# A second set of decoding buffers and eight more weight tiles for the first block of a fused attention, convolution and MLP kernel

## The chip, the cores and the metric

The kernel runs on one core of a Trainium2 chip. The metric is the device time of one execution in microseconds; the time before is the median of three runs, 1207.55 us (1206.89 to 1210.84). The engines are TensorE (PE, matmuls and transposes), VectorE (DVE), ScalarE (ACT), GpSimd (POOL) and SyncE (SP), which issues most of the DMAs here.

## What is computed

Three stages one after the other over 8 x 576 = 4608 tokens of width 512: attention within chunks of 64 tokens, a gated causal convolution, and a normalised two-layer network with a residual. Inputs q, k, v and g_ln are float32. All the weights are float64, because they are multiplied by a numpy scalar. In short form:

```
scores = scale * np.matmul(q_c, k_c.transpose(0, 1, 2, 4, 3))      # chunks of 64
attn = np.exp(scores - np.max(scores, axis=-1, keepdims=True))
attn = attn / (np.sum(attn, axis=-1, keepdims=True) + 1e-09)
x = heads_to_columns(np.matmul(attn, v_c))                        # 8 x 576 x 512
gate_pre += conv_w[k][None, None, :] * xp[:, k:k + S, :]          # k = 0..4
gate = 1.0 / (1.0 + np.exp(-gate_pre))
y = (gate * (x @ w_val)) @ w_out
xn = (y - mu) / np.sqrt(var + 1e-06) * g_ln
out = y + np.maximum(xn @ w_ch1, 0.0) @ w_ch2                     # hidden width 2048
```

## The kernel before

**Weights.** A float64 weight arrives as pairs of 32-bit words. decode (line 103) makes a float32 of each: one ACT operation on the high word (L106) and three integer operations on DVE (L107, L108, L109). split (line 111) then makes the two parts that PE multiplies, in fp32r: a rounded copy on ACT (L114) and the remainder by a subtraction on POOL (L115). Each product of two matrices is three matmuls, high by high, high by low and low by high. The raw words lie in the pool stg under the tag "raw" (two buffers), the decoded tile under the tag "da" (three buffers). The rows that the normalisation reads (load_rows, line 335) use the tag "da" too.

**Stages.** The tokens are cut into 36 units of 128 and nine blocks of 512. slot(u) (line 585) issues the loads of q, k and v of unit u+2, transposes q and k of unit u, and finishes unit u-2. The convolution, the value product and the output product of a block (tile names cg, psv, pso) are handed out over the slots that follow it, by the table dense. The order of PE in the first seven slots is that of the code (manual schedule); later a planner places the instructions. Behind slot(2), cwr takes the decoded convolution weights (20 rows) and g_ln (4 rows), and one transpose turns them into cw, which the convolution reads (L613 to L617).

After the last unit, prep(t) for t=0 to 3 normalises the rows of block 0 in pairs (ln_pair, line 341) into xn0, loads yt0 (the same rows, for the residual), and loads and splits the weight pairs f=0 to 3 of the network (load_ff, split_ff). A pair f is 128 of the 2048 hidden columns: w1 of it (512 x 128) and w2 of it (128 x 512).

**First block.** The loop at L673 runs over the 16 hidden tiles: ff1(0, f) is 12 matmuls psh<-xn,w, then hh on ACT and hl on DVE; ff2(0, f-1) is 12 matmuls into four accumulators acc. Behind them stands load_ff/split_ff of f+4. The w1 tiles turn over in four places of wA, so w1 of f+4 takes the place of w1 of f. Each decoded w1 tile is also stored to a scratch tensor (ad, L154). At f=4, 6, 8 and 10 ln_pair normalises two of the eight tiles of rows of the next two blocks into xt.

**Pairs.** The other eight blocks go two at a time (s=0 to 3) through eight pairs of hidden tiles; each pair is seven products of half matrices (zy, x) in place of eight, from seven sums of the weights (wc, built by make_pair from the scratch tensor) and seven right-hand operands (b21, b11, b22, t1 to t4, built in place on xt by right_operands, pool xb). Here the order of PE is that of the code again.

SP issues in its own order, one instruction after the other, and an instruction that waits for a buffer holds what is behind it.

## Time and profile before

| | us |
|---|---|
| median of three runs | 1207.55 |
| lowest, highest | 1206.89, 1210.84 |
| the profiled execution | 1211.44 |
| its span (first to last instruction) | 1209.7 |
| PE busy | 1124.9 (93%) |
| DVE busy | 739.4 (61%) |
| ACT busy | 529.6 (44%) |
| POOL busy | 159.8 (13%) |

The profile's times are from the start of the span. In a row of a timeline the first number is the start, the second the time that the row's instructions took, xN how many there are, and the brackets name how long the engine stood idle ahead of it and what ended that. "out<-in" are tile names. PEclk is the granted clock of TensorE as a share of its full 2.4 GHz.

### The profile page before, as it was taken

Reading aid. Unit: us, or ns where it says so; the run is one execution under the profiler, and the core shown is the slowest. Engines: PE = TensorE matmul, PEld = TensorE weight load, DVE = VectorE, ACT = ScalarE, POOL = GpSimd, SP = SyncE. Lnnn points to the kernel's source line nnn. Section 1 sums busy time; section 2 is a strip of 40 time slices with the busy share of each in tenths; the row PEclk is TensorE's granted clock in tenths of the full one; section 3 lists DMA queues with packets and bytes.
Section 4 is the critical chain, followed back from the end, with each engine's and each line's share of the span. In section 5 each row is a group of like instructions: output and inputs, shape, how many; then the busy total and the mean of one; then the engine's idle time right before and its main releaser. Section 6 shows DMA issues by size and latency. Waiting matters only on the chain.

```text
span 1209.7 us, 18324 instructions
## 1 busy us (share of the span) xinstructions
PE 1124.9 (93%) x7127; PEld 903.8 (75%) x7127; DVE 739.4 (61%) x1244; ACT 529.6 (44%) x973; POOL 159.8 (13%) x160
## 2 busy tenths in 40 slices
PE   6689999999999977769999999999999999999998
PEld 5567777777777754547888778888888887887876
DVE  6688898888885776575554654343844436543333
ACT  4467677677666445443443422332323423222221
POOL 2131131111112322333231000000000000000000
PEclk8789999999999988789999999999999999999999
DMA  7745664444024553454343263323443332622212
GB/s 181 177 98 146 187 181 119 114 121 123 36 70 141 181 168 112 158 198 174 122 140 122 87 227 105 105 97 107 156 162 105 120 106 79 234 88 87 88 36 78
DMA packets 168908, 155.37 MB, mean 128 GB/s; under 512 B 120670, under 2 KB 128886, under 8 KB 168822
## 3 DMA queue, kind: packets, MB, share of 16 engines
q1 hardware_dynamic: 163638, 144.76, 39.5%
q10 hardware_dynamic: 5184, 9.44, 2.1%
q8 instruction: 56, 0.92, 0.3%
q14 instruction: 30, 0.25, 0.1%
HBM read 116.41 MB, written 37.75 MB: 127 GB/s over the span
## 4 chain that ended last, share of the span: by engine, by line
PE 49%; DVE 5%; DMA 2%; POOL 1%; issue 1%; ACT 1%; SPq 0%; POOLq 0%; DVEq 0%; ACTq 0%
PE acc L497 13%; PE x L522 13%; PE psf L497 13%; PE zy L522 8%; DVE h L532 1%; POOL wc L407 1%; DVE xt L459 1%; PE pst L365 1%; DMA raws<-ad 1%; DVE yt L502 1%; DMA yr<-yd 1%; DVE t L407 1%; DMA out<-yr 0%; ACT h L531 0%; PE acc L399 0%
## 5 line engine op out<-in xcount | busy, mean ns | idle before, releaser
L540 DVE TENSOR_TENSOR c<-x,c 128x512 f32<-128x512 f32 x96 | 66.2, 689 | 234.4 <-ACT c L536 179.9
L497 PE MATMUL acc<-w,h 128*128 128x512 f32 x768 | 186.1, 391 | 0.0
L497 PE MATMUL psf<-w,h 128*128 128x512 f32 x768 | 186.0, 391 | 0.0
L497 PEld LDWEIGHTS acc<-w,h 128*128 128x128 f32 x768 | 144.2, 188 | 31.4
L497 PEld LDWEIGHTS psf<-w,h 128*128 128x128 f32 x768 | 144.2, 188 | 31.3
L522 PE MATMUL x<-t,wc 128*128 128x512 f32 x576 | 148.3, 393 | 3.3 <-DVE c L540 3.3
L536 ACT ACTIVATE c<-zy 128x512 f32<-128x512 f32 x96 | 57.9, 604 | 193.2 <-PE zy L522 193.1
L522 PEld LDWEIGHTS x<-t,wc 128*128 128x128 f32 x576 | 108.8, 189 | 27.9 <-DVE c L540 4.6
L531 ACT ACTIVATE h<-c 128x512 fp32r<-128x512 f32 x96 | 60.5, 631 | 133.5 <-DVE c L540 133.1
L276 DVE SCALAR_TENSOR_TENSOR cg<-xf,cw,cg 128x516 f32<-128x516 f32 (+1 forms) x176 | 117.7, 716 | 0.3
L522 PE MATMUL zy<-b,wc 128*128 128x512 f32 x384 | 100.5, 397 | 2.1 <-ACT wc L406 1.9
L502 DVE TENSOR_TENSOR yt<-psf,yt 128x512 f32<-128x512 f32 x128 | 88.0, 690 | 23.0 <-PE psf L497 19.1
L522 PEld LDWEIGHTS zy<-b,wc 128*128 128x128 f32 x384 | 71.7, 190 | 18.0 <-ACT wc L406 2.4
L532 DVE SCALAR_TENSOR_TENSOR h<-c,h 128x512 fp32r<-128x512 f32 x96 | 68.4, 713 | 12.4 <-ACT h L531 12.1
L264 POOL TENSOR_TENSOR xl<-xf,xh 128x512 fp32r<-128x512 f32 (+1 forms) x40 | 51.3, 1287 | 164.1 <-ACT xh L263 164.1
L290 PE MATMUL pso<-oh,gh 128*128 128x512 f32 x144 | 60.0, 416 | 8.2 <-ACT gh L307 5.8
L290 PE MATMUL psv<-xh,vh 128*128 128x512 f32 x144 | 59.9, 417 | 5.3 <-DVE gv L304 4.0
L115 POOL TENSOR_TENSOR w<-da,w 128x512 fp32r<-128x512 f32 x32 | 46.0, 1440 | 123.2 <-ACT w L114 93.4
L407 POOL TENSOR_TENSOR wc<-raws,wc 128x256 fp32r<-128x256 f32 x56 | 47.5, 871 | 103.6 <-ACT wc L406 103.4
L290 PE MATMUL psv<-xl,vh 128*128 128x512 f32 x144 | 58.2, 404 | 0.8 <-POOL xl L264 0.8
L290 PE MATMUL psv<-xh,vl 128*128 128x512 f32 x144 | 58.1, 403 | 0.0
L522 PE MATMUL zy<-t,wc 128*128 128x512 f32 x192 | 50.9, 400 | 6.9 <-ACT wc L406 6.5
(108 smaller groups left out, 1799.7 us busy)
## 6 DMA issues: line engine op xcount, KB each, us to landing
wc<-wc SPq DMA_DIRECT2D x112, 512.0 KB, 3.2
raw<-in_moe_w_ch SPq DMA_DIRECT2D x32, 512.0 KB, 3.9
yr<-yd SPq DMA_DIRECT2D x52, 256.0 KB, 3.3
vr<-in_v SPq DMA_DIRECT2D x144, 64.0 KB, 2.5
yd<-y ACTq DMA_DIRECT2D x36, 256.0 KB, 2.8
kr<-in_k SPq DMA_DIRECT2D x64, 128.0 KB, 2.9
qr<-in_q SPq DMA_DIRECT2D x64, 128.0 KB, 2.9
out<-yt SPq DMA_DIRECT2D x20, 256.0 KB, 3.1
```

The lines of the kernel that those rows point to most:

```text
L115: (eng or nc.gpsimd).tensor_tensor(out=lo, in0=a, in1=hi, op=ALU.subtract)
L264: nc.gpsimd.tensor_tensor(out=xl[j][:, :, lo:hi], in0=src, in1=xh[j][:, :, lo:hi], op=ALU.subtract)
L276: nc.vector.scalar_tensor_tensor(out=o, in0=x[:, f, i + lo:i + hi], scalar=cw[:, i * CT + f:i * CT + f + 1], in1=o, op0=ALU.mult, op1=ALU.add,
L290: nc.tensor.matmul(out=ps, lhsT=lt, rhs=rh, start=(i == 0), stop=(i == n - 1))
L407: eng.tensor_tensor(out=lo, in0=a, in1=hi, op=ALU.subtract)
L497: nc.tensor.matmul(out=ps, lhsT=lt, rhs=rh, start=(g == 0 and k == 0 and (first or half)), stop=(g == 1 and k == 2 and (last or half)),)
L502: nc.vector.tensor_tensor(out=yt[i], in0=ps, in1=yt[i], op=ALU.add)
L522: nc.tensor.matmul(out=ps, lhsT=lt, rhs=rh, start=(start and c == 0 and i == 0), stop=(c == 1 and i == 2), skip_group_check=True)
L531: nc.scalar.activation(out=t[:, 0, :], in_=src, func=ACTF.Relu)
L532: nc.vector.scalar_tensor_tensor(out=t[:, 1, :], in0=src, scalar=0.0, in1=t[:, 0, :], op0=ALU.max, op1=ALU.subtract)
L536: nc.scalar.activation(out=t, in_=zy, func=ACTF.Copy)
L540: nc.vector.tensor_tensor(out=t, in0=x, in1=t, op=ALU.add)
```

## The change

- g_ln gets a tile of its own, gr, in the pool of constants. It is loaded right behind the convolution weights, ahead of the loads of unit 2, and transposed by a second small transpose. cwr then holds the 20 rows of the convolution alone.
- A second pool of staging buffers, stg2, with raw and da tiles of its own (two each), takes the odd f from f=5 on. The even f stay in stg.
- w1 of f=4 to 7 go to a new pool w1p and those of f=12 to 15 to a new pool w3p; f=0 to 3 and 8 to 11 share the four places of wA. These pools and stg2 hold memory that the right-hand operands (xb) use later; they are closed behind ff2 of f=15, and xb opens then. It used to open ahead of the loop.
- The loop runs two more pairs ahead: next_ff(4) and next_ff(5) stand before it, and next_ff(f+6) in it.
- ln_pair becomes ln_rows, which takes its rows. Block 0 is normalised in one call of four tiles, from yt0 itself; yt0 is overwritten by that and loaded a second time. For xt, each pair of tiles has a tile "y" of its own in stg2, at f=3, 5, 7 and 9.
- make_pair(0) stands ahead of right_operands(), and both outside the manual order.
- split loses the choice of engine for the subtraction, which was always POOL.

The core of the diff:

```diff
+    gr = const.tile([CT, P], F32, name="gr")
...
-    def split(hi, lo, raw, eng=None):
-        a = stg.tile([P, DM], F32, tag="da", name="da", bufs=3)
+    def split(hi, lo, raw, pool=None):
+        a = (pool or stg).tile([P, DM], F32, tag="da", name="da", bufs=3)
...
-    def load_ff(f):
-        r1 = stg.tile([P, DM, 2], U32, tag="raw", name="raw1")
+    def load_ff(f, pool):
+        r1 = pool.tile([P, DM, 2], U32, tag="raw", name="raw1", bufs=2)
...
-    def split_ff(f):
+    def split_ff(f, pool):
         r1, r2 = wraw.pop(f)
-        t = wA.tile([P, 2, DM], F32R, tag=f"s{NFA + f % NFA}", name=f"w0_{f}")
-        a = split(t[:, 0, :], t[:, 1, :], r1)
+        g, m = divmod(f, NFA)
+        if g % 2 == 0:
+            t = wA.tile([P, 2, DM], F32R, tag=f"s{NFA + m}", name="w0")
+        else:
+            t = p2[f"w{g}"].tile([P, 2, DM], F32R, tag=f"w{m}", name="w0")
+        a = split(t[:, 0, :], t[:, 1, :], r1, pool)
...
-    def ln_pair(s, i):
-
-        ys = [load_rows(s, i + t) for t in range(2)]
+    def ln_rows(ys, i):
...
+    nc.sync.dma_start(out=gr, in_=g_ln.rearrange("(c p) -> c p", p=P))
...
-    cwr = stg.tile([(KC + 1) * CT, P], F32, tag="da", bufs=3, name="cwr")
-    nc.sync.dma_start(out=cwr[KC * CT:(KC + 1) * CT, :], in_=g_ln.rearrange("(c p) -> c p", p=P))
-    decode(cwu, cwr[0:KC * CT, :])
+    cwr = stg.tile([KC * CT, P], F32, tag="da", bufs=3, name="cwr")
+    decode(cwu, cwr)
     ps = ps_t.tile([P, NP * P], F32, tag="t", name="pst")
-    nc.tensor.transpose(out=ps[:, 0:(KC + 1) * CT], in_=cwr, identity=ident[0:(KC + 1) * CT, 0:(KC + 1) * CT])
+    nc.tensor.transpose(out=ps[:, 0:KC * CT], in_=cwr, identity=ident[0:KC * CT, 0:KC * CT])
+    nc.tensor.transpose(out=ps[:, KC * CT:(KC + 1) * CT], in_=gr, identity=ident[0:CT, 0:CT])
...
-            nc.sync.dma_start(out=yt0, in_=y_dram[0].rearrange("(t p) d -> p t d", p=P))
-        if t % 2 == 0:
-            ln_pair(-1, t)
-            src = p2["xt"][:, :, t * P:(t + 2) * P]
-            hi, lo = (x[:, :, t * P:(t + 2) * P] for x in xn0)
-            nc.scalar.activation(out=hi, in_=src, func=ACTF.Copy)
-            nc.vector.tensor_tensor(out=lo, in0=src, in1=hi, op=ALU.subtract)
-        load_ff(t)
-        split_ff(t)
+            y0 = y_dram[0].rearrange("(t p) d -> p t d", p=P)
+            nc.sync.dma_start(out=yt0, in_=y0)
+            ln_rows([yt0[:, i, :] for i in range(HB)], 0)
+            nc.sync.dma_start(out=yt0, in_=y0)
+            for i in range(0, HB, 2):
+                ts = slice(i * P, (i + 2) * P)
+                high_low(xn0[0][:, :, ts], xn0[1][:, :, ts], p2["xt"][:, :, ts], nc.vector)
+        load_ff(t, stg)
+        split_ff(t, stg)
...
-    p2["xb"] = ctx.enter_context(tc.tile_pool(name="xb", bufs=1, reuse_waits="tile"))
+    s_1 = ExitStack()
+    p2["w1"] = s_1.enter_context(tc.tile_pool(name="w1p", bufs=1, reuse_waits="tile"))
+    stg2 = s_1.enter_context(tc.tile_pool(name="stg2", bufs=2, reuse_waits="tile"))
+    p2["w3"] = s_1.enter_context(tc.tile_pool(name="w3p", bufs=1, reuse_waits="tile"))
+
+    def next_ff(f):
+        if NFA <= f < NF:
+            pool = stg2 if f % 2 else stg
+            load_ff(f, pool)
+            split_ff(f, pool)
+
+    def rows_of(s, i, t):
+        for k in range(2):
+            nc.sync.dma_start(out=t[:, k, :], in_=rows(s, i + k)[0])
+        return [t[:, k, :] for k in range(2)]
+
+    next_ff(NFA)
+    next_ff(NFA + 1)
     for f in range(NF):
         ff1(0, f)
         if f > 0:
             ff2(0, f - 1)
-        if f + NFA < NF:
-            load_ff(f + NFA)
-            split_ff(f + NFA)
-        if f in (4, 6, 8, 10):
-            ln_pair(0, f - 4)
+        next_ff(f + NFA + 2)
+        if f in (3, 5, 7, 9):
+            ln_rows(rows_of(0, f - 3, stg2.tile([P, 2, DM], F32, tag="y", name="yr")), f - 3)
     ff2(0, NF - 1)
-    right_operands()
+    s_1.close()
+    p2["xb"] = ctx.enter_context(tc.tile_pool(name="xb", bufs=1, reuse_waits="tile"))
     s_0.close()
     p2["hr"] = ctx.enter_context(tc.tile_pool(name="p2r", bufs=5, side="right", reuse_waits="tile"))
     p2["wx"] = ctx.enter_context(tc.tile_pool(name="p2w", bufs=1, side="right", reuse_waits="tile"))
     p2["c"] = ctx.enter_context(tc.tile_pool(name="pc", bufs=2, reuse_waits="tile"))
     p2["yt"] = ctx.enter_context(tc.tile_pool(name="pyt", bufs=2, reuse_waits="tile"))
+    make_pair(0)
+    right_operands()
     order = ExitStack()
     order.enter_context(tc.manual_schedule(engines={mybir.EngineType.PE}))
-    make_pair(0)
```

SP at the head, from the load of the convolution weights (cwu) on: the loads of units 2, 3 and 4, and g_ln. Before:

```order
L575 DMA cwu<-in_moe_conv_w 20x256
L88 DMA kr<-in_k 128x4x64 x2
L88 DMA qr<-in_q 128x4x64 x2
L97 DMA vr<-in_v 64x4x64 x4
L88 DMA kr<-in_k 128x4x64 x2
L88 DMA qr<-in_q 128x4x64 x2
L97 DMA vr<-in_v 64x4x64 x4
L88 DMA kr<-in_k 64x4x64 x4
L88 DMA qr<-in_q 64x4x64 x4
L97 DMA vr<-in_v 64x4x64 x4
L613 DMA cwr<-in_moe_g_ln 4x128
```

After:

```order
L579 DMA cwu<-in_moe_conv_w 20x256
L580 DMA gr<-in_moe_g_ln 4x128
L89 DMA kr<-in_k 128x4x64 x2
L89 DMA qr<-in_q 128x4x64 x2
L98 DMA vr<-in_v 64x4x64 x4
L89 DMA kr<-in_k 128x4x64 x2
L89 DMA qr<-in_q 128x4x64 x2
L98 DMA vr<-in_v 64x4x64 x4
L89 DMA kr<-in_k 64x4x64 x4
L89 DMA qr<-in_q 64x4x64 x4
L98 DMA vr<-in_v 64x4x64 x4
```

The load of g_ln moved from behind the loads of three units (32 instructions) to a place ahead of them.

DVE in the first block, between the hl of f=1 and that of f=2. Before, raw1_4936 and raw2_4938 are the weights of f=4:

```order
L384 SCALAR_TENSOR_TENSOR hl_4971<-psh_4957,hh_4970 128x512
L109 SCALAR_TENSOR_TENSOR da_4941<-raw1_4936,da_4941 128x512
L107 TENSOR_SCALAR da_4950<-da_4950 128x512
L108 SCALAR_TENSOR_TENSOR da_4950<-raw2_4938,da_4950 128x512
L109 SCALAR_TENSOR_TENSOR da_4950<-raw2_4938,da_4950 128x512
L384 SCALAR_TENSOR_TENSOR hl_5025<-psh_5011,hh_5024 128x512
```

After, raw1_5071 is w1 of f=8, and raw1_4929 and raw2_4931 are the pair f=5:

```order
L388 SCALAR_TENSOR_TENSOR hl_5002<-psh_4988,hh_5001 128x512
L110 SCALAR_TENSOR_TENSOR da_5076<-raw1_5071,da_5076 128x512
L108 TENSOR_SCALAR da_4934<-da_4934 128x512
L109 SCALAR_TENSOR_TENSOR da_4934<-raw1_4929,da_4934 128x512
L110 SCALAR_TENSOR_TENSOR da_4934<-raw1_4929,da_4934 128x512
L108 TENSOR_SCALAR da_4943<-da_4943 128x512
L109 SCALAR_TENSOR_TENSOR da_4943<-raw2_4931,da_4943 128x512
L110 SCALAR_TENSOR_TENSOR da_4943<-raw2_4931,da_4943 128x512
L108 TENSOR_SCALAR da_5085<-da_5085 128x512
L388 SCALAR_TENSOR_TENSOR hl_5056<-psh_5042,hh_5055 128x512
```

At the same place of the loop DVE now works on pairs that are used later, and on two chains of buffers in turn (f=8 in stg, f=5 in stg2).

DVE around the last hl (f=15; in the order after, those of f=12 to 14 stand right ahead of it). b21, b11, b22 and t3 are right-hand operands, raws the sums of the weights for pair 0, yt0 the first block's output. Before, with the end of the decode of the last weight tile among it:

```order
L107 TENSOR_SCALAR da_5672<-da_5672 128x512
L108 SCALAR_TENSOR_TENSOR da_5672<-raw2_5660,da_5672 128x512
L384 SCALAR_TENSOR_TENSOR hl_5780<-psh_5766,hh_5779 128x512
L109 SCALAR_TENSOR_TENSOR da_5672<-raw2_5660,da_5672 128x512
L407 TENSOR_TENSOR b22_5821<-xt_4563,b22_5821 128x1024
L431 TENSOR_TENSOR raws_5861<-raws_5860 128x256
L459 TENSOR_TENSOR xt_4563<-xt_4563 128x2x512
L402 TENSOR_TENSOR yt0_4575<-acc_4974,yt0_4575 128x512
L402 TENSOR_TENSOR yt0_4575<-acc_4975,yt0_4575 128x512
L402 TENSOR_TENSOR yt0_4575<-acc_4976,yt0_4575 128x512
L402 TENSOR_TENSOR yt0_4575<-acc_4977,yt0_4575 128x512
```

After:

```order
L388 SCALAR_TENSOR_TENSOR hl_5678<-psh_5664,hh_5677 128x512
L388 SCALAR_TENSOR_TENSOR hl_5707<-psh_5693,hh_5706 128x512
L388 SCALAR_TENSOR_TENSOR hl_5736<-psh_5722,hh_5735 128x512
L388 SCALAR_TENSOR_TENSOR hl_5765<-psh_5751,hh_5764 128x512
L411 TENSOR_TENSOR b21_5849<-xt_4565,b21_5849 128x1024
L411 TENSOR_TENSOR b11_5852<-xt_4565,b11_5852 128x1024
L406 TENSOR_TENSOR yt0_4577<-acc_5005,yt0_4577 128x512
L406 TENSOR_TENSOR yt0_4577<-acc_5006,yt0_4577 128x512
L406 TENSOR_TENSOR yt0_4577<-acc_5007,yt0_4577 128x512
L406 TENSOR_TENSOR yt0_4577<-acc_5008,yt0_4577 128x512
L411 TENSOR_TENSOR b22_5855<-xt_4565,b22_5855 128x1024
L463 TENSOR_TENSOR xt_4565<-xt_4565 128x2x512
```

The weights' last decode and the weight sums of pair 0 now stand ahead of these rows; b21 and b11, which stood among the decodes before, come right behind it.

## Rows read from the trace of the kernel before

**Rows 1.** Windows: from:to, length, busy time of PE, PEld, DVE, ACT, POOL, clock.

```profile
110.00:170.00 60.00, 55.30 (x677) 43.64 (x676) 53.44 (x90) 43.48 (x72) 13.78 (x14) 1.00 0.66 174
240.00:340.00 100.00, 96.11 (x1090) 77.05 (x1082) 85.92 (x141) 69.84 (x114) 17.56 (x17) 1.00 0.33 87
...
427.00:515.00 88.00, 65.39 (x232) 46.79 (x231) 55.97 (x101) 42.40 (x89) 24.74 (x18) 0.83 0.44 144
515.00:537.00 22.00, 12.38 (x39) 8.55 (x38) 19.18 (x34) 11.59 (x22) 8.10 (x9) 0.76 0.48 172
560.00:600.00 40.00, 39.40 (x177) 32.49 (x177) 21.11 (x40) 15.61 (x36) 10.22 (x14) 1.00 0.37 132
```

**Rows 2.** Timeline of PE at the head.

```profile
36.78 0.27 PE L616 MATMUL pst<-ident,cwr 24*128 24x24 f32 x1 [9.05 <-DMA cwr<-in_moe_g_ln]
...
44.45 0.60 PE L172 MATMUL pst<-ident,kr 128*128 128x128 f32 x4
44.89 0.60 PE L172 MATMUL pst<-ident,qr 128*128 128x128 f32 x4
```

**Rows 3.** Timeline of SP's queue at the head.

```profile
29.46 2.57 SPq L88 DMA_DIRECT2D qr<-in_q  x4
...
34.77 0.45 SPq L613 DMA_DIRECT2D cwr<-in_moe_g_ln  x1
```

**Rows 4.** The page's DMA issues: count, KB each, median us to landing.

```profile
qr<-in_q SPq DMA_DIRECT2D x64, 128.0 KB, 2.9
```

**Rows 5.** Timeline of PE, first block.

```profile
380.33 5.76 PE L290 MATMUL psh<-xn,w 128*128 128x512 f32 x24
...
388.70 2.96 PE L290 MATMUL psh<-xn,w 128*128 128x512 f32 x12
...
405.44 2.96 PE L290 MATMUL psh<-xn,w 128*128 128x512 f32 x12
```

**Rows 6.** Timeline of SP's queue, first block: two loads of w1, three pairs apart.

```profile
391.73 0.38 SPq L142 DMA_DIRECT2D raw<-in_moe_w_ch  x1
...
414.22 0.38 SPq L142 DMA_DIRECT2D raw<-in_moe_w_ch  x1
```

**Rows 7.** Waits of PE, 427 to 515: us in total, times, longest.

```profile
PE acc L399 <- ACT w L114: 7.5, 3, 3.7
PE pst L365 <- ACT yr L362: 6.4, 2, 6.0
PE acc L399 <- POOL w L115: 3.6, 4, 2.0
```

**Rows 8.** Groups of DVE, 380 to 427: count, busy us, mean ns, idle before.

```profile
L109 DVE SCALAR_TENSOR_TENSOR da<-raw,da 128x512 uint32<-128x512 uint32 x12 | 13.6, 1136 | 0.3
L108 DVE SCALAR_TENSOR_TENSOR da<-raw,da 128x512 uint32<-128x512 uint32 x11 | 7.6, 691 | 0.3
L107 DVE TENSOR_SCALAR da<-da 128x512 uint32<-128x512 uint32 x11 | 6.7, 612 | 11.0 <-ACT da L106 10.9
```

**Rows 9.** Timeline of DVE and POOL in the first block.

```profile
400.08 1.73 POOL L115 TENSOR_TENSOR w<-da,w 128x512 fp32r<-128x512 f32 x1 [3.00 <-ACT w L114]
400.70 1.66 DVE L109 SCALAR_TENSOR_TENSOR da<-raw,da 128x512 uint32<-128x512 uint32 x1
```

**Rows 10.** Timeline of PE: first product behind the first block, and pair 1.

```profile
514.42 2.05 PE L522 MATMUL x<-b,wc 128*128 128x512 f32 x6
...
536.49 1.52 PE L522 MATMUL zy<-b,wc 128*128 128x512 f32 x6
```

**Rows 11.** Waits of PE, 515 to 537.

```profile
PE zy L522 <- ACT wc L406: 6.5, 1, 6.5
PE x L522 <- DVE c L540: 2.7, 2, 1.5
```

**Rows 12.** Groups of DVE, 427 to 540: right-hand operands, and a small operation.

```profile
L407 DVE TENSOR_TENSOR t<-xt,t 128x1024 fp32r<-128x1024 f32 x4 | 4.9, 1218 | 0.0
...
L357 DVE TENSOR_TENSOR w<-w,ve 128x2 f32<-128x2 f32 x5 | 0.8, 162 | 0.2
```

11 lines of the change are left out of this document (6 added, 5 removed).

## The prediction

> **What bounds the kernel now.** I read the windows first, to find where TensorE (PE) is not full, and then, inside each hole, the waits and the timeline. The last rows of the windows [rows 1] show a kernel that PE bounds where its data is there: 39.40 of 40 us at 560 to 600. Three stretches are not like that. At the head PE stands 9.05 us still until the vector g_ln has landed [rows 2]. In the first block's network PE has 65.39 of 88 us at 427 to 515, at a granted clock of 0.83 [rows 1]. And in the change to the pairs of products it has 12.38 of 22 us. All three lie on PE's own order, and behind them PE is full to the end, so what is saved there moves the end by as much.
>
> In the first block one hidden tile f costs PE two sets of 12 matmuls: the sets for f=2 and for f=5 start at 388.70 and 405.44, three periods of 5.58 us [rows 5]. The supply is slower: the loads of a weight pair are issued at 391.73 and, three pairs on, at 414.22, 7.5 us each [rows 6], because the two raw buffers are refilled only when the pair ahead is decoded. Each pair so costs 1.9 us of the lead that the first four pairs gave, and from 427 on PE waits for weights (ACT's copy 7.5 us, POOL's subtraction 3.6) and for the normalised rows, 6.4 [rows 7]. The long waits also cost the clock (0.83 and 0.76 there against 1.00 at 240 to 340, [rows 1]).
>
> **The change part by part.**
>
> g_ln. Its load goes from behind the q, k and v loads of three later units to a place ahead of them, and into a tile of its own. Before, it is issued at 34.77 [rows 3], PE waits until 36.78 and had been free since 36.78-9.05=27.73 [rows 2]. That wait goes. What is late next is the q of unit 4: its four loads are issued from 29.46 on and take 2.57 us of the queue, and 2.9 us to land [rows 3, 4], so it is there at 29.46+2.57+2.9=34.9. PE wants it at 44.89 now [rows 2], at 35.8 with the wait gone: it fits by 0.9 us. So the gain is at most 9.05; I take 8.5. The lower end is 4.5: SP's queue is not sped up (it gains only the 0.45 us of the moved issue), and any later load that has no slack gives some back. The second small transpose is 0.27 us or less [rows 2] and lies in what was the wait: nothing.
>
> Attention. The rows of block 0 no longer hold the decoding buffers from early on, so all of f=0 to 3, and parts of 4, 6 and 8, are decoded beside attention: 11 tiles in place of 4, so seven more. A decode is a tile of L107, L108 and L109 on DVE, 0.61+0.69+1.14=2.44 us [rows 8], with a copy on ACT and a subtraction on POOL. Price: the stretch with the four decodes of before, 110 to 170, has PE busy 55.30 of 60, and at the rate of 240 to 340 (96.11 of 100) it would be 57.67 [rows 1]. That is 2.4 us for four, 0.6 each, 7x0.6=4.2 lost. The ends are nothing (DVE has 14 us idle in each 100 at 240 to 340) and 7x1.99=14 (all of a decode that meets no POOL work, 0.61+0.69+0.69 with L109 at the length of L108, as if DVE were full). I take 4.2, from the only stretch with decodes beside attention.
>
> End of attention. The rows of block 0 are now taken from yt0, in one normalisation of four tiles, and yt0 is loaded a second time since it is overwritten. That adds 1 MB on SP's queue and takes away four row loads of 256 KB; PE's first psh matmul follows the last output product directly, at 380.33 with no wait [rows 5]. I count nothing; if the normalisation ended later than the output product, PE would wait for the difference.
>
> First block. Eight more weight tiles and the second set of buffers give two more pairs of lead and two chains of load and decode, and rows have tiles of their own. PE's part is 16x5.58=89.3 us, and eight sets of transposes for the next rows, 0.44 each (44.45 to 44.89, [rows 2]): 92.8. Supply: from the hl of f=1 to that of f=10, DVE now has 19 decodes, 9 hl, 11 statistics and some 32 small operations: 19x2.44+20x0.69+32x0.16=65.3, against 9x5.58+3=53.2 on PE (hl and statistics as long as L108, which has their tile, and the small ones as the 0.16 of L357, [rows 12]: estimates). With 1.99 for a decode it is 56.7. DVE, in order, so holds PE back by 3.5 to 12 us. I take 8, the middle: seven decodes fewer are left for this stretch, but POOL works all through it. The first block then takes 92.8+8=100.8 in place of 514.42-380.33=134.1 [rows 5, 10]: 33.3 gained.
>
> Transition. The right-hand sums need the place of the eight tiles, so the pool for them opens only after the last ff2, and the weights of pair 0 are now made ahead of them, during hh9 to hh11. Now: 514.42 to 536.49, 22.1 us, of which 6.5 wait for weights and 2.7 for DVE's additions [rows 10, 11], so six products take 12.9, or 2.15 each at the low clock. After: b21 is no longer multiplied ahead of ff2(15), so seven products, 15.0; the additions again 2.7. The 6.5 wait goes, but t1 is late next: DVE must do one yt addition, the low part of b22, t3, the addition c, t1, t3's low part, t2 and t1's low part, 6x1.22+2x0.69=8.7 [rows 12], while PE needs 2x2.15=4.3 for b21 and b11. So 4.4 of wait takes its place: 15.0+2.7+4.4=22.1. Nothing is gained; its ends are -5 (seven products at the 6x5.58/24=1.4 us of the steady first block, since no long wait of PE goes before) and +6.5 (a wait as long as the one that goes, on top).
>
> Sum: -8.5+4.2-33.3+0=-37.6. Against the profiled execution (1211.44, its span 1209.7 and 1.7 around it) that is 1173.8; that execution was 3.9 above the median of 1207.55, so I forecast 1170.
>
> **Rivals.**
>
> DVE becomes the bound. One row shows it: with POOL's subtraction at 400.08, L109 at 400.70 takes 1.66 us, and POOL 1.73 [rows 9]. If the faster supply makes every one of the 19 decodes meet a subtraction, they cost 0.61+0.69+1.66=2.96, and DVE needs 19x2.96+18.9=75.1, so 22 over PE rather than 8: 1170+14=1184. For it: mean L109 is 1.14, so about half meet one already. Against it: they are not more in number than before, only closer. The Trainium skill's page "SBUF — State Buffer", section "Who interferes with whom", states that a DVE instruction with two SBUF inputs contends with a GpSimd (POOL) instruction that reads SBUF, that the lock is exclusive, and that issue order decides which of the two blocks; by it, what is decoded faster is paid for in more meetings, and the time would be that of this rival. The trace agrees in kind: L109 at 400.70, which came later, is held to 1.66 against the 0.69 of L108.
>
> Supply is complete. If decodes run mostly without collisions (8 falls to 3.5), cost attention nothing and the clock stays high through the transition: 1170-4.5-4.2-5=1156. For it: from 388.70 to 405.44 [rows 5] the decodes run beside three tiles at no loss to PE. Against: the new order of DVE puts the steps of three decodes and more between two hl.
>
> The queue turns it over. SP issues in order; in attention the weight loads and the stores of the decoded tiles stand between the q, k and v loads, and each waits for a buffer or a decode, with PE's own inputs queued behind it. If a decode is late by more than the two units of lead, PE loses a unit; a unit is some 9.4 us (36 of them in the first 340 us, an estimate). Four such losses, 38 us, take away the whole gain; seven of them, one for each decode added, give 1170-4.2+66=1232, slower. For it: the queue has about a dozen such instructions more in attention. Against: the four decodes of before cost 2.4 us in all.
>
> The change delivers less at head and in attention than I take: 4.5 rather than 8.5, and 14 rather than 4.2: 1170+4+10=1184, inside the range.
>
> **How the numbers follow.** My forecast has 0.59, DVE as the bound 0.13, complete supply 0.12, less at the head and in attention 0.11, the queue 0.05. The predicted time is 1170, with a range from 1152 (complete supply, and DVE holding nothing back) to 1188 (DVE as the bound, or less at the head and in attention, and a little for both together); the queue's case is left out. A measurement of this kernel can tell about 0.3% (3.6 us) from no change. All cases but the queue are faster; four of the queue's losses bring it within 0.3%, more of them over, so faster 0.95, same 0.02, slower 0.03.
>
> **What would show it.** Head: no wait of PE in front of the two small transposes, and unit 4 some 9 us earlier. Attention: DVE busier, PE a few us less per 100. First block: sets of 12 matmuls 5.6 to 6.2 us apart through all 16 tiles, no wait over 2 us on ACT's w or on the rows, clock near 1.00. Transition: the wait on ACT's wc replaced by one on the low part of t1. It is wrong if PE waits for q, k or v in attention, if DVE is full and hl late in the first block, or if b21 comes late after the last ff2.

## The result, and the profile of the changed kernel

The changed kernel takes 1196.25 us (median of five runs, 1193.61 to 1201.02) against 1210.63 us of the kernel before (five runs): a ratio of 0.9899, with a 95% interval of 0.9867 to 0.993. It is faster by some 13 us; 37.6 were forecast, and the time lies outside the range. The profiled execution is the fastest of the five (1193.61 us, span 1191.8). By stages, both spans laid side by side (starts of PE's rows, as in [rows 5, 10]):

| stretch | before | after | moved | forecast |
|---|---|---|---|---|
| start to the first psh | 380.33 | 378.60 | -1.7 | -4.3 |
| first block, to the first product of pair 0 behind it | 134.1 | 114.95 | -19.1 | -33.3 |
| transition, to pair 1 | 22.1 | 25.75 | +3.7 | 0 |
| from there to the end | 673.2 | 672.5 | -0.7 | 0 |
| span | 1209.7 | 1191.8 | -17.9 | -37.6 |

Before, one of the seven products of pair 0 (zy<-b, at 505.00) lies inside the first block; after, all seven lie in the transition.

**Windows** of the changed kernel: from:to, length, busy time of PE, PEld, DVE, ACT, POOL (in brackets the instructions), clock; the last two columns, the DMA's share and GB/s, are not used here. They answer to [rows 1].

```profile
110.00:170.00 60.00, 55.80 (x615) 43.98 (x614) 52.81 (x88) 43.68 (x73) 14.50 (x15) 0.97 0.67 170
240.00:340.00 100.00, 96.13 (x1081) 77.11 (x1079) 85.96 (x140) 69.51 (x114) 18.05 (x17) 1.00 0.35 93
378.00:415.00 37.00, 27.97 (x120) 22.09 (x119) 32.51 (x48) 18.72 (x33) 17.22 (x12) 0.97 0.56 185
427.00:494.00 67.00, 59.16 (x259) 47.39 (x259) 41.28 (x82) 31.45 (x70) 19.44 (x17) 0.97 0.38 130
494.00:519.00 25.00, 13.46 (x41) 9.18 (x40) 20.29 (x20) 10.71 (x20) 12.09 (x10) 0.79 0.53 190
```

The end of the first block is better than before (59.16 of 67 us, at a clock of 0.97 for 0.83). But there is a new hole at its beginning, 27.97 of 37 us, where DVE is busy for 32.51; and the transition is as thin as it was.

**Head.** Timeline of PE, changed kernel; the first two rows answer to [rows 2], and the last two stand later in the head.

```profile
27.47 0.23 PE L620 MATMUL pst<-ident,cwr 20*128 20x20 f32 x1
27.55 0.20 PE L621 MATMUL pst<-ident,gr 4*128 4x4 f32 x1
...
64.02 0.66 PE L219 MATMUL pst<-ident,pr 128*128 128x128 f32 x4 [3.79 <-ACT kT L178]
...
76.71 0.90 PE L219 MATMUL pst<-ident,pr 128*128 128x128 f32 x3 [6.38 <-ACT kT L178]
```

The wait of 9.05 us is gone: the load of g_ln passed the loads of units 2 to 4 (28, as the rows of the order show, not 32), and unit 3 starts 9.3 us earlier than before. Then part of the wait comes back. Unit 7 is 7.6 us earlier, unit 9 only 3.4. The two rows wait for ACT's copies kT, and ACT's queue and DVE's at that time read so (columns as above):

```profile
74.26 1.91 ACT L288 ACTIVATE cg<-cg 128x2048 f32<-128x2048 f32 x1
76.08 0.58 ACT L178 ACTIVATE kT<-pst 128x512 f32<-128x512 f32 x1
```

```profile
34.00:75.00 41.00, 26.56 (x380) 21.84 (x378) 37.80 (x66) 22.82 (x44) 12.16 (x12) 0.83 0.71 174
```

The copy stands behind the gate's activation L288, and that reads the convolution cg, which DVE makes; the second fence is a row of windows (as above): DVE has 37.80 of 41 us of work. Before, it had 5.00 us of work from 28 to 44 and was full from 44 to 80, 35.24 of 36 us (windows of the kernel before):

```profile
28.00:44.00 16.00, 7.22 (x99) 6.57 (x100) 5.00 (x9) 4.97 (x10) 1.53 (x2) 0.68 0.52 116
44.00:80.00 36.00, 28.14 (x382) 22.74 (x380) 35.24 (x63) 22.47 (x44) 13.36 (x12) 0.86 0.70 174
```

So the wait for g_ln lay ahead of a queue of DVE work, and without it PE meets that queue.

**First block.** Waits of PE from 340 to 540 (us in total, times, longest), which answer to [rows 7, 11]:

```profile
PE pst L369 <- ACT yr L366: 13.9, 4, 6.0
PE x L526 <- DVE c L544: 4.2, 2, 3.4
PE zy L526 <- ACT t L410: 3.9, 1, 3.9
PE zy L526 <- DVE t L411: 3.1, 1, 3.1
PE acc L403 <- DVE hl L388: 3.0, 1, 3.0
```

No wait for a weight is left (14.0 us before in the same window, 11.1 of them from 427 to 515). The waits for the rows rose from 6.4 to 13.9. The longest is this one, in the timelines of SP, DVE, POOL and PE:

```profile
389.66 0.42 SPq L690 DMA_DIRECT2D yr<-yd  x1
...
395.24 0.42 SPq L690 DMA_DIRECT2D yr<-yd  x1
```

```profile
397.29 0.68 DVE L352 BATCH_NORM_STATS2 s<-yr 128x6 f32<-128x512 f32 x1
...
401.65 0.68 DVE L352 BATCH_NORM_STATS2 s<-yr 128x6 f32<-128x512 f32 x1
402.25 1.70 DVE L109 SCALAR_TENSOR_TENSOR da<-raw,da 128x512 uint32<-128x512 uint32 x1
...
409.03 1.24 DVE L362 TENSOR_SCALAR w<-w 128x2 f32<-128x2 f32 x1
...
411.79 1.22 DVE L364 SCALAR_TENSOR_TENSOR w<-mv,r 128x2 f32<-128x2 f32 x1
```

```profile
402.13 1.27 POOL L116 TENSOR_TENSOR w<-da,w 128x512 fp32r<-128x512 f32 x1 [1.29 <-ACT w L115]
```

```profile
413.91 1.11 PE L369 MATMUL pst<-ident,yr 128*128 128x128 f32 x4 [6.04 <-ACT yr L366]
```

From the first statistic of the pair of rows (397.29) to the last small operation (413.01) DVE needs 15.7 us. The chain itself is 11 operations of some 2.8 us when nothing meets them (two statistics of 0.68, nine small ones of about 0.16); between them stand the decodes of weights for tiles that PE reaches later. The two loads of rows landed at 392.4 and 399.7, ahead of their statistics, so the rows wait in DVE's queue and not for the load. DVE issues in order, and TensorE's order has the transposes in the middle of ff1 of f=5: PE stands. The row at 402.25 also shows a meeting with POOL (a DVE operation that begins beside a subtraction of POOL and takes longer for it), as [rows 9] did: 1.70 us.

Behind the waits the granted clock falls as well. Windows of the whole first block, before (first row) and after, and of the 8 us behind the long wait:

```profile
380.33:514.42 134.09, 110.01 (x423) 82.31 (x422) 88.72 (x144) 61.06 (x121) 43.21 (x31) 0.89 0.50 160
378.60:493.55 114.95, 98.08 (x417) 78.32 (x416) 84.04 (x149) 58.03 (x120) 40.97 (x32) 0.96 0.48 157
412.00:420.00 8.00, 6.09 (x19) 5.09 (x20) 7.09 (x11) 5.28 (x14) 3.55 (x3) 0.57 0.67 195
```

PE stood idle for 24.1 us before and for 16.9 after, and the granted clock was on its lower level (1.2 GHz) for 29.6 us before and for 10.2 after. Eight psh matmuls take 3.76 us on that level (from 415.96, behind the long wait) and 2.12 on the upper one (from 431.32). An estimate from these rows: of the 19.1 us gained, 7.2 are idle time, some 8.5 the clock (0.44 of 19.4), and some 2 the product that moved into the transition.

The groups of DVE from 382 to 450 (count, busy us, mean ns, idle before), which answer to [rows 8, 12]:

```profile
L110 DVE SCALAR_TENSOR_TENSOR da<-raw,da 128x512 uint32<-128x512 uint32 x19 | 20.7, 1096 | 0.1
L109 DVE SCALAR_TENSOR_TENSOR da<-raw,da 128x512 uint32<-128x512 uint32 x19 | 16.0, 845 | 0.2
L108 DVE TENSOR_SCALAR da<-da 128x512 uint32<-128x512 uint32 x20 | 9.3, 465 | 10.4 <-ACT da L107 10.4
L362 DVE TENSOR_SCALAR w<-w 128x2 f32<-128x2 f32 x3 | 1.5, 516 | 0.0
```

A decode is 1.10+0.85+0.47=2.41 us, as forecast (2.44). But L362, an operation on two elements, takes 0.52 on average instead of 0.16, and 10.4 us of idle time stand at the beginning: DVE waits for ACT's copy of a weight until 382. From then on it is nearly full, and its last decode ends at 455.94, while PE starts ff1 of f=15 only at 485.24: DVE works ahead of PE, and the rows and low parts that PE wants first stand among these decodes.

**Transition.** PE, changed kernel (answers to [rows 10]):

```profile
493.55 1.52 PE L526 MATMUL zy<-b,wc 128*128 128x512 f32 x6
494.91 1.52 PE L526 MATMUL x<-b,wc 128*128 128x512 f32 x6
500.32 0.50 PE L526 MATMUL zy<-t,wc 128*128 128x512 f32 x1 [3.89 <-ACT t L410]
503.89 2.50 PE L526 MATMUL zy<-t,wc 128*128 128x512 f32 x5 [3.07 <-DVE t L411]
...
513.98 1.80 PE L526 MATMUL x<-t,wc 128*128 128x512 f32 x6 [3.38 <-DVE c L544]
```

The wait for wc is gone, and PE waits for the right-hand operands t instead: 3.89+3.07, and 0.42 more behind them, then 4.2 for c. DVE makes these operands beside POOL's low parts of wc, and its operations on 128x1024, 1.22 us in [rows 12], take 1.74 to 1.76 from 498.75 to 507.2 (timelines of POOL and DVE):

```profile
497.01 9.10 POOL L411 TENSOR_TENSOR wc<-raws,wc 128x256 fp32r<-128x256 f32 x6 [28.56 <-ACT wc L410]
500.41 1.75 DVE L463 TENSOR_TENSOR xt<-xt 128x1024 f32<-128x1024 f32 x1
```

### The profile page after: what moved, and what is told of

The parts are those of the page before. It is cut to its first block, busy times and chain, and to the rows that moved or that the text cites. A ratio compares the mean times of both kernels' runs of the same rounds, so it can differ in the third digit from the quotient of the medians.

```text
span 1191.8 us, 18298 instructions
## 1 busy us (share of the span) xinstructions
PE 1114.5 (94%) x7128; PEld 902.3 (76%) x7128; DVE 738.2 (62%) x1237; ACT 527.4 (44%) x972; POOL 158.1 (13%) x160
## 3 DMA queue, kind: packets, MB, share of 16 engines
q1 hardware_dynamic: 163590, 144.76, 39.7%
## 4 chain that ended last, share of the span: by engine, by line
PE 61%; DVE 26%; ACT 5%; issue 3%; SPq 2%; DMA 1%; POOL 1%; DVEq 0%; POOLq 0%; ACTq 0%
PE acc L501 14%; PE x L526 14%; PE psf L501 14%; PE zy L526 9%; DVE cg L281 8%; PE psv L295 3%; DVE da L109 2%; DVE pr L211 2%; DVE da L110 2%; PE pso L295 2%; DVE sm L208 2%; PE psh L295 2%; DVE ex L202 1%; PE pst L369 1%; DVE mx L199 1%
## 5 line engine op out<-in xcount | busy, mean ns | idle before, releaser
L526 PEld LDWEIGHTS x<-t,wc 128*128 128x128 f32 x576 | 109.3, 190 | 29.6 <-DVE c L544 5.1
L536 DVE SCALAR_TENSOR_TENSOR h<-c,h 128x512 fp32r<-128x512 f32 x96 | 68.0, 709 | 13.1 <-ACT h L535 12.7
L295 PE MATMUL pso<-oh,gl 128*128 128x512 f32 x144 | 56.9, 397 | 0.7 <-DVE gl L313 0.7
```

What stands on the lines that cost most here:

```text
L295: nc.tensor.matmul(out=ps, lhsT=lt, rhs=rh, start=(i == 0), stop=(i == n - 1))
L526: nc.tensor.matmul(out=ps, lhsT=lt, rhs=rh, start=(start and c == 0 and i == 0), stop=(c == 1 and i == 2), skip_group_check=True)
L536: nc.vector.scalar_tensor_tensor(out=t[:, 1, :], in0=src, scalar=0.0, in1=t[:, 0, :], op0=ALU.max, op1=ALU.subtract)
```

## The experiments

All were timed against the kernel before in the same session, and none leaves out work. The changed kernel was not timed again in these sessions, so a difference to it lies across sessions, in which the median of the kernel before was 1209.3 to 1211.3 us. Ratios have 95% intervals; the first block is read as above, from the first psh to the first product of pair 0.

### The head: E1 and E4

E1 is the kernel before with g_ln's tile alone.

```diff
+    gr = const.tile([CT, P], F32, name="gr")
...
+    nc.sync.dma_start(out=gr, in_=g_ln.rearrange("(c p) -> c p", p=P))
...
-    cwr = stg.tile([(KC + 1) * CT, P], F32, tag="da", bufs=3, name="cwr")
...
+    cwr = stg.tile([KC * CT, P], F32, tag="da", bufs=3, name="cwr")
...
```

> The kernel before with g_ln's own tile and early load, and nothing else. As predicted (PE's own wait is the price): the time falls by 8.5 us, and unit 9 and all later units stand 8 to 9 us earlier. New theory, DVE bounds the head from about 44 us on: units 3 to 7 stand 9 to 10 us earlier, but what is left behind the convolution of block 0 (unit 9 on) is what DVE gained, 3 to 5 us, and the time falls by 3 to 5 us.

Measured: 1204.77 us, ratio 0.995 (0.9935 to 0.9964), so 6.0 us. Unit 6 is 9.9 us earlier than before, unit 9 only 3.1, much as in the changed kernel (10.5 and 3.4), which has all the other edits. Giving back is therefore a matter of the head itself. E4 moves the decodes of w_out (four tiles) at the head: they are handed out at slot 8 and not at slot 5.

```diff
-    at(0, (5, 1), lambda: split_w("o"))
+    at(0, (8, 0), lambda: split_w("o"))
```

> The changed kernel with the decode of w_out (4 tiles, some 7 us of DVE) handed out at unit 8 in place of unit 5. If DVE is the bound of the head, the convolution and the gate of block 0 end earlier, and unit 9 stands up to 7 us earlier than in the changed kernel; of this some is lost when the decode comes, so the time falls by 0 to 5 us. If ACT's order (k's copy behind the gate) is the bound and not DVE's work, unit 9 does not move by more than 1 us.

Measured: 1188.17 us, 0.9818 (0.9794 to 0.9842), 8.1 below the changed kernel. Unit 9 is 12.0 us earlier than before, and unit 35 still 6.3. The last operation of the convolution of block 0, first in the changed kernel and then in E4:

```profile
72.21 0.47 DVE L281 SCALAR_TENSOR_TENSOR cg<-xf,cw,cg 128x256 f32<-128x256 f32 x1
60.20 0.48 DVE L281 SCALAR_TENSOR_TENSOR cg<-xf,cw,cg 128x256 f32<-128x256 f32 x1
```

What is late next at the head is DVE's convolution; the load of q was not. And it is late by the order on DVE rather than by the amount of its work: the decodes of w_out still run at the head (operations L109 and L110 from 61.26 on in place of 57.46), and from 34 to 75 DVE is as full in E4 (39.07 us for 37.80), but the convolution stands ahead of them, and the gate's activation starts at 60.71 in place of 74.26.

### Later rows, and the subtraction on VectorE: E2, E3, E5, E8

E2 moves the normalisation of the rows two tiles later.

```diff
-        if f in (3, 5, 7, 9):
...
+        if f in (5, 7, 9, 11):
...
```

> The changed kernel with the four normalisations of the next rows at f=5, 7, 9 and 11 in place of 3, 5, 7 and 9; all work is still done. Theory, DVE is overloaded up to about 460 us and idle after, and PE's transposes stand ahead of the rows: PE's waits for the normalised rows fall from 13.9 to under 6 us, and the time by 5 to 9 us. Rival, it is the amount of DVE's work between the hl that holds PE (weights late as well): the wait moves to the weights or to hl, and the time changes by less than 2 us.

Measured: 1193.31 us, 0.9862 (0.9839 to 0.9885); the interval overlaps that of the changed kernel. The waits for rows fall from 13.9 to 8.1, but 5.5 us of waits for hh and hl come in: rows and low parts stand in the same queue.

E3 takes POOL out of the first block: the low parts of the weights from f=4 on are subtracted on DVE, which so has more to do.

```diff
-        nc.gpsimd.tensor_tensor(out=lo, in0=a, in1=hi, op=ALU.subtract)
+        (nc.vector if pool is not None and p2.get("w") is not None else nc.gpsimd).tensor_tensor(out=lo, in0=a, in1=hi, op=ALU.subtract)
```

> The changed kernel with the subtraction of the low parts of the weights f=4 to 15 on DVE in place of POOL. It adds 24 operations of 0.69 us to DVE (16.6 us) and takes away the meetings with POOL. If a meeting costs DVE about 1.0 us on whatever it is doing (also on the two-element operations of the normalisation), some 21 meetings go, 20 us: DVE's busy time in the first block falls by 2 to 5 us and the time by 2 to 6 us. If meetings cost only the half of L110's lengthening (0.4 each, 9 us), DVE's work grows by 8 us and the time by 4 to 8 us.

Measured: 1175.19 us, 0.9705 (0.9686 to 0.9724), 21 below the changed kernel; the first block takes 95.6 us. Groups of DVE from 382 to 450 and a wait of PE from 366 to 530, E3:

```profile
L109 DVE SCALAR_TENSOR_TENSOR da<-raw,da 128x512 uint32<-128x512 uint32 x21 | 14.4, 695 | 0.0
L110 DVE SCALAR_TENSOR_TENSOR da<-raw,da 128x512 uint32<-128x512 uint32 x21 | 14.1, 681 | 0.0
```

```profile
PE pst L369 <- ACT yr L366: 2.3, 2, 1.2
```

The meetings with POOL's subtractions are gone (681 for 1096 ns). A decode with its subtraction is now 0.70+0.68+0.42+0.68=2.48 us of DVE's time, no less than 2.41: the decodes gained nothing. What fell is the time of the other operations, the small ones above all: in the whole first block DVE is busy for 76.7 us in place of 84.0, though it has 24 subtractions more. The chains of the second to fourth pair of rows, from the first statistic to the last small operation, take 9.5, 9.0 and 11.0 us in place of 14.2, 13.4 and 15.7. But the first pair's, which the longest wait hangs on, takes 17.3 in place of 15.7, with 23 operations of decoding and subtraction in between for 14, and it ends at nearly the same time (412.4 for 413.0); it is long by DVE's order and not by the meetings. What else moved is PE's order: the planner put the first transposes behind 6.6 tiles of ff1, where the changed kernel has 5.25. E3 so mixed two causes; E15 to E18 part them.

E5 makes the same edit on the kernel before.

> The kernel before, with the subtraction of the low parts of the weights f=4 to 15 on DVE in place of POOL. Theory, the kernel before is held by its two raw buffers and by POOL's link in the chain: the loads of a pair come closer than 7.5 us by less than 1 us, and the time falls by 3 to 9 us, much less than the 21 us that the same edit gave behind the change. Rival, meetings with POOL were the whole trouble already: the time falls by 15 us or more, and the change's buffers and tiles would be worth little.

Measured: 1203.22 us, 0.9949 (0.9929 to 0.9968): 6.3 us. The same edit is worth three times as much on the changed kernel.

E8 was to give DVE its work earlier: the second load of yt0 on ACT's queue, and the pools w3p and stg2 opened ahead of w1p (not shown in the cut).

```diff
-            nc.sync.dma_start(out=yt0, in_=y0)
+            nc.scalar.dma_start(out=yt0, in_=y0)
...
```

> The changed kernel with the second load of yt0 issued by ACT's queue in place of SP's (so it does not hold the loads of f=5), and with the pools of w1 for f=12 to 15 and f=4 to 7 in each other's place (so that the tile of f=4 does not lie where the last block's gated values are). All work is done. Theory A, DVE lost 10.2 us waiting at 372 to 382 and that is what PE waits for later: DVE's wait falls to under 4 us and the time by 5 to 9 us. Theory B, the meetings with POOL set the pace from 382 on and ACT's order holds the start anyway: the time changes by less than 3 us.

Measured: 1198.33 us, 0.9918 (0.9891 to 0.9945). DVE still stands idle for 10.5 us at the beginning: the copy it waits for (L107, at 388.28) was released by a subtraction of POOL, and the rounded copy ahead of that (L115, at 386.26) stands on ACT behind the last evictions of y. So the edit didn't do what it was for, and what an earlier start is worth stays open.

### Do they add? E6, E7, E11

E6 is E3 and E4 together; E7 has in addition the subtractions of all other weights on DVE; E11 is E7 with one pair less of lead.

```diff
-        next_ff(f + NFA + 2)
+        next_ff(f + NFA + 1)
```

> The changed kernel with both edits: the low parts of f=4 to 15 on DVE, and w_out decoded at unit 8. If the two are separate places on PE's path, the gains add up: 1196 less 21 less 8, 1166 to 1169. If what the head gains is given back in attention because DVE is full there, it stays at 1171 to 1176.

> As e6, but with the low parts of all weights on DVE, those of w_val, w_out and f=0 to 3 too (16 more operations of 0.69 us, 11 us, at the head and in attention, where DVE is the bound or nearly). If a meeting costs about 1.0 us there too, DVE gains some 5 us and the time falls by 0 to 5 us against e6. If few of them meet, it rises by 2 to 8 us.

> As e7, with pairs loaded five ahead in place of six. With the meetings gone the supply has slack, so the first block stays within 2 us, and what is not decoded beside attention gives 0 to 3 us. If the sixth pair of lead is still needed, the time rises by 2 to 6 us.

Measured: E6 1167.24 us (0.9662, 0.9642 to 0.9683), E7 1166.58 (0.9656, 0.9639 to 0.9673), E11 1167.33 (0.964, 0.9618 to 0.9663). E3's 21 and E4's 8 add to 29. At the head and in attention it makes no difference where the subtraction is done (E7 and E6 are within 1 us), and the sixth pair of lead is worth nothing in E7.

### The second set of buffers and the eight tiles: E9, E10, E12

E9 takes away the second set (only the rows' tiles stay in stg2), E10 the eight tiles (and with them the lead of two pairs, which has no place then), E12 both.

```diff
-            pool = stg2 if f % 2 else stg
+            pool = stg
```

```diff
-        g, m = divmod(f, NFA)
-        if g % 2 == 0:
-            t = wA.tile([P, 2, DM], F32R, tag=f"s{NFA + m}", name="w0")
-        else:
-            t = p2[f"w{g}"].tile([P, 2, DM], F32R, tag=f"w{m}", name="w0")
+        t = wA.tile([P, 2, DM], F32R, tag=f"s{NFA + f % NFA}", name="w0")
...
-        next_ff(f + NFA + 2)
+        next_ff(f + NFA)
```

> The changed kernel, but all f are loaded and decoded in the one set of buffers stg, as before the change; the rows keep their own tiles and the eight extra weight tiles stay. If the second chain of buffers is what gave the first block its gain, a pair again takes some 7 to 7.5 us, PE waits for weights (over 10 us) and the time rises by 6 to 14 us against the changed kernel. If DVE's meetings with POOL set the pace in any case, the time stays within 3 us of it.

> The changed kernel without the eight extra weight tiles: w1 turns over in the four places of wA again, pairs are loaded four ahead in place of six; the second set of buffers and the rows' own tiles stay. If lead is what counts, PE waits for weights and the time rises by 5 to 12 us against the changed kernel. If the pace of DVE counts and not the lead, the first block is as long within 3 us. Fewer weights are decoded beside attention, so the last unit stands 1 to 4 us earlier.

> The changed kernel without both of the things that gave the decoding more room: one set of decoding buffers, no eight extra weight tiles; the rows' own tiles, the rows from x as it was loaded, and g_ln's own tile stay. No work is left out. E10 (extra tiles away, second set kept) took 1169.4 us, E9 (second set away, extra tiles kept) 1185.0. Theory A (room lets the in-order VectorE work ahead on weights, and that is all that the second set does): the second set was worth -11 us beside the extra tiles and is worth nothing or less without them, so 1163 to 1173. Theory B (the second set is supply, and TensorE lacks it once the extra tiles are gone): the first block waits longer for low parts, 1176 to 1186.

| us (first block, transition) | tiles and lead as before | eight more tiles, two pairs more of lead |
|---|---|---|
| one set | E12 1177.2 (109.7, 13.1) | E9 1185.0 (104.1, 27.0) |
| two sets | E10 1169.4 (102.3, 13.1) | changed 1196.3 (115.0, 25.8) |

Ratios: E9 0.979 (0.9769 to 0.9812), E10 0.966 (0.9639 to 0.9682), E12 0.9738 (0.972 to 0.9757). Each of the two parts that the change is named after makes it slower where the other is present: the tiles with their lead cost 27 us with two sets and 8 with one, the second set costs 11 with the tiles and brings 8 without them. What is in E12 beside g_ln (the rows' own tiles, block 0 from yt0, make_pair ahead), which was not parted further, brings most of the gain: 32 us below before, 6 of them by E1.

With the tiles as before, the transition takes 13 us. Timelines of DVE (first row) and PE, E10:

```profile
460.81 3.48 DVE L407 TENSOR_TENSOR b<-xt,b 128x1024 fp32r<-128x1024 f32 x3
```

```profile
484.44 1.54 PE L522 MATMUL zy<-b,wc 128*128 128x512 f32 x6
485.82 1.52 PE L522 MATMUL x<-b,wc 128*128 128x512 f32 x6
487.18 1.52 PE L522 MATMUL zy<-t,wc 128*128 128x512 f32 x6
```

The right-hand operands are made from 460.81 on, beside the first block's last tiles; in the changed kernel their first subtraction starts at 489.82, since their place holds weights that ff1 reads to its end. What the tiles cost in the first block beside two sets (115.0 for 102.3) goes with places and lengths together, as the next runs show, and wasn't parted further.

In E9 the rows aren't waited for at all. The first statistic there is at 388.5 and the last small operation ends at 395.35, 6.8 us for the chain, with three operations of decoding in between in place of 14, at a mean of L110 that is hardly lower (1068 ns for 1096). PE's waits are for low parts, in small pieces (366 to 530, E9):

```profile
PE acc L403 <- DVE hl L388: 6.0, 6, 1.4
```

### Place or meetings: E15 to E18

PE's order in the first block is fixed by hand (the loop stands in manual order), and the transposes are issued by a call of their own, d tiles behind the statistics:

```diff
+            turns[f + d] = ln_rows(rows_of(0, f - 3, ...), f - 3, True)
+        if f in turns:
+            turns.pop(f)()
```

d=1 puts them behind 5 tiles of ff1 (near the changed kernel), d=3 behind 7 (near E3). E17 and E18 also have E3's edit.

> The changed kernel with TensorE's order in the first block fixed by hand: the transposes of the first rows of a pair of tiles stand behind 5 tiles of ff1 and 4 of ff2, and so on every second tile (the changed kernel has them at 5.2 and 4). Subtraction on GpSimd as in the changed kernel. No work is left out. It is the base of a square of four (early or late transposes, subtraction on GpSimd or on VectorE). Both theories: near the changed kernel, 1192 to 1200 us, and about 12 us of waits of TensorE for the rows.

> As E15, with the transposes two tiles later (behind 7 of ff1 and 6 of ff2; in E3 the planner had put them at 6.6 and 5, which I had overlooked). No work is left out. Theory A (the meetings of VectorE with GpSimd cost the first block its time): the wait moves to low parts, as in E2, within 5 us of E15. Theory B (E3's gain came from the later place of the transposes in TensorE's order): 12 to 18 us below E15.

> As E15, with the low parts of the weights from f=4 on subtracted on VectorE as in E3. No work is left out. Theory A: most of E3's gain without the later place, 14 to 20 us below E15. Theory B: within 5 us of E15, with the waits for the rows still near 10.

> Both: late transposes and the subtraction on VectorE, so near E3 (1175.2 us) by both theories. No work is left out. Theory A: within 5 us of E17. Theory B: within 5 us of E16. If each brings about half, both are needed.

| us (first block) | transposes early | late |
|---|---|---|
| subtraction on POOL | E15 1193.1 (111.3) | E16 1187.7 (108.2) |
| subtraction on DVE | E17 1185.0 (103.7) | E18 1174.6 (95.4) |

Ratios: E15 0.9857 (0.9831 to 0.9884), E16 0.9814 (0.9793 to 0.9835), E17 0.9796 (0.9775 to 0.9817), E18 0.9706 (0.968 to 0.9732). Neither theory holds alone: the place brings 5.4 us, the meetings 8.2, both 18.5. (The 4.9 us that both together bring over the sum are no more than the spread of four runs each can make.) Moving the subtraction takes POOL's link out of the chain of the weights too; PE waited for no weight in any of the four, but the two were not parted. The row of PE's waits from 366 to 530 that tells them apart, first of E15:

```profile
PE pst L349 <- ACT yr L376: 9.0, 3, 4.7
```

The same view of E16, where PE waits for no rows, but for low parts:

```profile
PE acc L408 <- DVE hl L393: 6.3, 5, 3.0
```

Of E17, where the rows are waited for once:

```profile
PE pst L349 <- ACT yr L376: 8.6, 1, 8.6
```

And of E18, where this is the only wait of the first block over 1 us in sum:

```profile
PE acc L408 <- DVE hl L393: 1.6, 2, 1.3
```

With the meetings, later rows only hand the wait to hl and hh (3.3 us for hh in E16). Without them, early rows still wait once, in the first pair, where DVE has begun its decodes late (8.9 us of idle time for ACT's copy stand in E17 from 382 to 450); that this is the reason wasn't parted. Its chain is not shorter without meetings (17.6 us in E17, 15.7 in E15); the waits that go with the meetings are the later ones, and the 3.0 for hl. Only together both waits go.

### All gains: E13 and E14

E13 is E10 with the edits of E7; E14 is E13 with one set.

> E10 (without the eight extra tiles, 1169.4 us) with every weight's low part on VectorE, as in E7, and w_out decoded later, as in E4. No work is left out. Theory A (three separate causes: the right operands' place, the meetings of VectorE with GpSimd, VectorE's load at the head): E4's edit gave -8.1 beside the change and the meetings of the first block, as far as E10 still has them, 5 to 10, so 1151 to 1157. Theory B (E10's and E3's gains are the same one, VectorE working ahead): only the head's 8 remain, less what they overlap, 1161 to 1167.

> E13 with one set of decoding buffers. No work is left out. Theory A (the second set only lets VectorE work ahead): within 3 us of E13, or below it. Theory B (it is supply): 5 to 12 us above E13, with TensorE's waits for low parts in the first block longer by that much.

Measured: E13 1152.60 us, 0.9534 (0.952 to 0.9548); E14 1161.25, 0.9609 (0.9593 to 0.9625). The right operands' place, the meetings and the order at the head are each worth something beside the other two, but they don't add in full: E10's 27 us and E6's 29 would give 1140. What overlaps is the first block, which E10 shortens by 12.6 us, E3 by 19.3, and E13 by 20.9 in all. Against E7, which differs by the tiles and lead, E13 is 14 us lower, and in the profiled runs nearly all of that is the transition (13.2 for 25.9; first block 94.1 for 95.8). The second set is worth 8.7 us in the medians here. That it is the supply that it was thought to be is not shown: in the profiled runs, which lie 4.0 apart, the first block is 2.0 us longer with one set and the waits for low parts are 2.9. Windows of E13:

```profile
380.00:420.00 40.00, 39.52 (x178) 31.54 (x177) 39.07 (x94) 26.58 (x57) 0.00 (x0) 1.00 0.78 254
420.00:460.00 40.00, 39.80 (x181) 32.13 (x180) 38.40 (x75) 28.37 (x57) 9.20 (x6) 1.00 0.42 136
```

PE and DVE are both full, DVE more than in the changed kernel (77.5 of 80 us for 73.3), and PE loses nothing. So a full DVE alone does not hold PE back here.

## Why the prediction was wrong, step by step

**g_ln, -8.5: wrong.** The wait went, and the bound of the lower end (4.5, queue of SP) named the wrong queue. "What is late next is the q of unit 4" failed: it is DVE's convolution, which stands in DVE's order among decodes and softmax (E4). Three units later 3.1 us of E1's 9.9 are left; of the whole, E1 kept 6.0, which lies between the stated ends, but not for the stated reason. In the changed kernel 4.2 are left at unit 17. What DVE had to do behind the wait stood in the timeline of before, and it wasn't read.

**Attention, +4.2: right in kind, and near by luck in size.** From unit 17 to unit 35 the changed kernel loses 3.7 us against before, and eleven tiles are decoded beside attention, as counted. 3.0 of the 3.7 are idle time of PE (10.4 us for 7.4; new are 4.8 of waits for DVE's gv). The rest goes with 3.4 us in which the granted clock was 0.5, for which the forecast had no term; before had none. The other kernels that decode the same eleven tiles there lose between 3.8 us (E12, with the same 3.4 us) and 9.4 (E8, with 17.1 us at 0.5). The windows at 240 to 340 are as before because the eleven decodes lie between 146 and 238.

**End of attention, 0: right within 1.2 us** (unit 35 starts 0.5 us earlier than before, the first psh 1.7), and the first psh comes without a wait; the second load of yt0 is held until 367.38 and the first load of rows issued at 389.66.

**First block, -33.3: this is the step that failed.** PE's 92.8 us was right (E18 has 95.4, E13 94.1). Of supply, the load was right too: from the hl of f=1 to that of f=10 DVE was busy 66.9 us, 65.3 forecast. The sum came out in part by luck: each operation counted until the next one starts, the decodes took 41.7 us (46.4 forecast), 36 small operations 10.0 (5.1), and four sums of weights, which had no term, 3.0. But the step took 8 from a range that ended at 12, which was its own sum (65.3 against 53.2), and treated DVE as a rate. The stretch took 71.4 us (387.97 to 459.33), 18.2 over PE's. As a rate, DVE was not what held PE: in that stretch it decoded every tile that was left, up to f=15, where PE had come to f=10, and over the whole block it was busy for 84.0 of 114.95 us, in E13 for 85.1 of 94.1. The reasons are the order on DVE, in which decodes for later tiles stand ahead of rows and low parts; the place of the transposes in PE's order, which the prediction didn't look at; the meetings, which lengthen the later chains of rows; and perhaps the idle 10.4 us ahead. The square shows the place and the meetings, and E9 against E3 the order (6.8 us for the first chain with three operations of decoding in between, 17.3 with 23); the share of the late beginning stays open (E8). What the waits then cost is more than their own 16.9 us, since the clock falls behind them: 92.8+16.9 and some 4.5 for the clock (an estimate, 0.44 of 10.2) is 114.2 of the 114.95. "Clock near 1.00" among the signs held behind 465 only.

**Transition, 0: a size was off.** The mechanism was right, a wait for t in place of wc. The forecast had 4.4+2.7=7.1 us of waits, there are 11.6 (7.4 for t, 4.2 for c); the change cost 3.7, inside the ends. Of the 3.0 that t took more, 1.6 are three of DVE's operations ahead of the last release (503.89) at 1.75 us in place of 1.22, beside POOL, and 1.4 are PE, which did b21 and b11 in 2.9 us and not in 4.3 and so began to wait earlier. What was missed is the other side: without the tiles, the same make_pair ahead and rows would have brought 9 us there (13.1, E10, at a clock of 1.00). The change gave that away for tiles that brought nothing with one set or with two.

**The rivals.** "DVE becomes the bound" (1184) is the nearest: its place and its 22 us over PE are what the first block shows (114.95 less 92.8). Its mechanism, every decode met, is not: a decode had 2.41 us, not 2.96, and E13 shows DVE as full as that at no loss to PE. "Less at the head and in attention" (1184 too) came true in part: up to the first psh the change brought 1.7 us in place of 4.3. "The queue turns it over" wasn't seen: no unit was lost. "Complete supply" (1156) wasn't reached by this change; E13, which has less room for weights, is below it.

## What to carry to other kernels

More buffers and more lead don't only supply: an engine that issues in order then works ahead, and what the bounding engine wants next can wait behind what it wants later. So for each wait that an edit removes, look up the next wanted operation in the order of its engine, with the place where its reader stands, before dividing an engine's load by time. And ask of every tile what held its place before: eight tiles that kept a later stage's operands out cost more (14 us in E13 against E7, with their lead) than they could save.

## What the runs showed of the hardware

A meeting with POOL lengthens even the smallest operations of DVE, by up to 1.1 us. In the changed kernel from 382 to 460, of the operations that stand alone in the timeline, 19 of L109 and L110 began with POOL idle and took 0.67 to 0.69 us; 14 began during a subtraction of POOL and took 1.17 to 1.79; three began in its last 0.06 us and took 0.68. Operations on two elements with two inputs, or of the form of L355 and L362 (tensor_scalar), took 0.14 to 0.17 with POOL idle and up to 1.29 when they began during a subtraction, as the rows of L362 and L364 above (1.24, 1.22): eight times their length, in the middle of a chain that PE waits for. Not lengthened were hl, which has one input in PSUM (0.68 to 0.69, three of 11 during a subtraction), and the statistics, with one input (0.65 to 0.68, two of nine); in E10 from 384 to 475 nine hl began during a subtraction and took 0.68 on average.

The Trainium skill's "SBUF — State Buffer", section "Who interferes with whom", says that two SBUF inputs make a DVE instruction contend with a POOL instruction that reads SBUF, that a mode which a tensor_scalar can enter contends with POOL too, and that one with at most one SBUF input outside that mode doesn't. The trace agrees in each of these groups. Priced in the prediction as a load on each decode, the rule gave 1184; the runs show that it falls on the short operations of a chain as well: between the hl of f=1 and that of f=10 forty of them took 12.6 us in E15 and 3.8 in E17, each counted until the next operation starts, while the decodes with their subtraction took 42.8 us in E17 and without it 39.7 in E15.
